# Last channel group, gated values and output products: from weight order over four batches to the order of two batch pairs

## Chip, core and metric

The kernel runs on one core of one Trainium2 chip. The metric is the device time of one execution in microseconds (us). Engines are named as in the profile: PE multiplies matrices, PEld loads their weights, DVE and POOL work on whole tiles, ACT applies functions, SP issues transfers.

## What is computed

Four batches, 448 positions, width 768 (12 heads of 64). Three parts follow each other:

```python
scores = scale * q @ k.T - log(S)
x = sigmoid(scores) @ v                       # attention, heads side by side: (4, 448, 768)

u = x + mix(x)                                # low-rank mixing over positions
y = u + relu(u @ w_ch1) @ w_ch2               # channel products, 768 -> 3072 -> 768

gate_pre[:, s] = sum_k conv_w[k] * y[:, s - 4 + k]    # 5 taps over positions
out = (sigmoid(gate_pre) * (y @ w_val)) @ w_out       # values, then outputs
```

Inputs are fp32, the weights arrive as float64 bits.

## The kernel before

Everything is held transposed: 768 channels are KC = 6 blocks of 128 partitions, and one tile of a batch b and block m is 128 x 448. A product of fp32 precision is made of three matmuls per block of 128 (`mm3`, line 173): weight high x data high, weight high x data low, weight low x data high. So every operand exists as a high part (a copy by ACT) and a low part (a subtraction by DVE or POOL).

The order of instructions on each engine is the order of the program (`tc.manual_schedule`, line 623). Within one engine nothing is passed. Products go through eight PSUM banks in turn.

Weights. There are 120 half weights of 128 x 384: halves 0 to 95 belong to the channel products (twelve groups of eight), 96 to 107 to the six value weights, 108 to 119 to the six output weights. `prep_half` (142) makes the next half ready: four DVE operations unpack the float64 bits (lines 83, 84, 85, 88), one flush later ACT copies the high part (73), and one flush after that DVE subtracts for the low part (75). `prep_half` itself begins with a flush, and so does each product. It also issues the load of the half three later (138, raw ring of three tiles). Prepared halves lie in a pool of ten tiles (`2 * WS`), except for the first three. A product may take its weight in parts: the second half of a weight is first touched by the 10th of 18 matmuls, its low part by the 12th.

Channel groups (570). Group g takes two first products per batch (`ch1`, 371: 18 matmuls, relu by ACT on line 374, low part by DVE on 375) and, per batch and block, one second product (`ch2`, 380: 6 matmuls, added to x by DVE on 387). In the last group `y_split` (389) also splits each finished y: high by ACT (392), low by POOL (393).

Gates (`gate_steps`, 396). Each of the 24 tiles (b, m) goes through five steps: two taps scaled by ACT and added by POOL (410), a third tap scaled by ACT and added by POOL (414), the fourth tap by one DVE operation (417), the fifth by another that writes over y, a sigmoid by ACT (426). `before(i)` and `after(i)` run these steps for several tiles at once, so that each call of the pair moves one tile forward by a step and starts another.

Values (597). For each weight m and each batch b: `val` (429) is a product of 18 matmuls, and DVE multiplies it into the gate (432). After the last weight `z_split` (434) splits the gated tiles: ACT high (73), DVE low (77). An output product `fin` (439, 18 matmuls) needs all six split tiles of its batch; ACT copies it out (441), and SP sends it.

Operand tiles (y, split y, gate, gated and output tiles) share a ring of 32.

By the end of the last group 103 halves are prepared, so seven halves of value weights; ten more follow during the 24 value products, one for every two products.

Of the kernel before, what the change touches and what calls it, by code (L numbers as in the profile page):

```python
# [8 lines left out]
F32 = mybir.dt.float32  # L9
F32R = mybir.dt.float32r  # L10
# [6 lines left out]
P = 128  # L17
B, H, S, D = 4, 12, 448, 64
# [3 lines left out]
KC = DM // P  # L22
NF = DFF // P
G = 2
NG = NF // G
# [4 lines left out]
HQ = DM // 2  # L30
# [2 lines left out]
WS = 5  # L33
LAG = 2
EARLY = 3


@with_exitstack
def tile_kernel(
# [18 lines left out]
    nc = tc.nc  # L58
# [4 lines left out]
    def flush(every=False):  # L63

        while deferred:
            now, deferred[:] = deferred[:], []
            for part in now:
                part()
            if not every:
                return  # L70
# [8 lines left out]
    def unpack(raw, a, x):  # L79


        low, high = raw[:, :, 0], raw[:, :, 1]
        nc.vector.tensor_scalar(a, f32(high), 2.0 ** -112, None, op0=ALU.mult)
        nc.vector.tensor_scalar(x, low, 2.0 ** -29, 7.0, op0=ALU.mult, op1=ALU.min)
        nc.vector.scalar_tensor_tensor(
            x, a.bitcast(U32), 3, x, op0=ALU.logical_shift_left, op1=ALU.bitwise_or
        )
        nc.vector.scalar_tensor_tensor(  # L88
            x, high, 0x80000000, x, op0=ALU.bitwise_and, op1=ALU.bitwise_or
        )  # L90
# [13 lines left out]
    def operand(name, dt=F32R):  # L104
        return op_p.tile([P, 2, S], dt, tag="op", name=name)

    def scratch(name):
        return operand(name, F32)[:, :, :].rearrange("p t s -> p (t s)")
# [5 lines left out]
    def x_of(b, m):  # L114
        return xs[:, m, b, PAD:]
# [7 lines left out]
    pools = {}  # L123
# [5 lines left out]
    def load_half():  # L129
# [3 lines left out]
        n, half = divmod(i, 2)  # L133
        if i < EARLY:
            r = scratch(f"raw{i}")[:, :2 * HQ].bitcast(I64)
# [6 lines left out]
    def prep_half():  # L142
        i = at["prep"]
        if i >= 2 * len(sources):
            return
        flush()
        n, half = divmod(i, 2)
        if i < EARLY:
            t = operand(f"w{i}")[:, :, :HQ]
            ax = operand(f"x{i}", F32)  # L150
            a, x = ax[:, 0, :HQ], ax[:, 1, :HQ].bitcast(U32)
        else:
            t = pools["w"].tile([P, 2, HQ], F32R, tag="w", name=f"w{i}")[:, :, :]
            a = pools["a"].tile([P, HQ], F32, tag="a", name=f"a{i}")[:, :]
            x = pools["a"].tile([P, HQ], U32, tag="x", name=f"x{i}")[:, :]
        wt.setdefault(n, []).append(t)
        unpack(wraw.pop(i), a, x)

        def high():
            split(f32(x), t[:, 0], t[:, 1], later=True)  # L160
            deferred.append(lambda: ready.add(i))

        deferred.append(high)
        at["prep"] += 1
        if i >= EARLY:
            load_half()
# [204 lines left out]
    def ch1(c, b):  # L371
        ps = product(f"ch1_{c}_{b}", weight(c // G * 2 * G + c % G), lambda k: us[b, k])
        t = operand(f"h{c}_{b}")
        nc.scalar.activation(t[:, 0], ps, AF.Relu)  # L374
        nc.vector.scalar_tensor_tensor(  # L375
            t[:, 1], ps, 0.0, f32(t[:, 0]), op0=ALU.max, op1=ALU.subtract
        )
        hs[c, b] = t

    def ch2(g, b, m):  # L380
        flush()
        ws = [weight((2 * g + 1) * G + i) for i in range(G)]
        ps = bank(f"ch2_{g}_{b}_{m}")
        for i in range(G):
            mm3(ps[:, :S], ws[i], m, hs[g * G + i, b], i == 0, i == G - 1)
        y = x_of(b, m)
        nc.vector.tensor_add(y, ps[:, :S], y)  # L387

    def y_split(b, m):
        y = x_of(b, m)  # L390
        t = operand(f"y{b}_{m}")
        nc.scalar.activation(t[:, 0], y, AF.Copy)  # L392
        nc.gpsimd.tensor_sub(t[:, 1], y, f32(t[:, 0]))  # L393
        ys[b, m] = t

    def gate_steps(b, m):

        t = []
        y = xs[:, m, b]
        z = x_of(b, m)  # L400
        tap = lambda k: f32(cw[:, m * TAPS + k:m * TAPS + k + 1])

        def scaled(dst, k):
            nc.scalar.activation(dst, y[:, k:k + S], AF.Copy, scale=tap(k))

        def first():
            t.append(operand(f"g{b}_{m}", F32))
            scaled(t[0][:, 0], 0)
            scaled(t[0][:, 1], 1)
            nc.gpsimd.tensor_add(t[0][:, 0], t[0][:, 0], t[0][:, 1])  # L410

        def second():
            scaled(t[0][:, 1], 2)
            nc.gpsimd.tensor_add(t[0][:, 0], t[0][:, 0], t[0][:, 1])  # L414

        def fused(dst, k):
            nc.vector.scalar_tensor_tensor(
                dst, y[:, k:k + S], tap(k), t[0][:, 0], op0=ALU.mult, op1=ALU.add
            )

        return (
            first,
            second,
            lambda: fused(t[0][:, 0], 3),
            lambda: fused(z, 4),
            lambda: nc.scalar.activation(z, z, AF.Sigmoid),
        )
# [6 lines left out]
    def z_split(b, m):  # L434
        t = operand(f"z{b}_{m}")
        split(x_of(b, m), t[:, 0], t[:, 1])
        zs[b, m] = t
# [29 lines left out]
    def attention_phase(att, kq_scope, raw_scope):  # L467
# [15 lines left out]
        def weights(i):  # L483
            if i < EARLY:
                load_half()
# [37 lines left out]
    def main_phase(tail):  # L523
        mix = iter(tail)

        def take(n):
            for _ in range(n):
                next(mix)()

        flush(every=True)  # L530
        ch1(0, 0)
        take(1)
        settle(0)
        yield
        prep_half()
        ch1(0, 1)
        take(NSC)
        prep_half()
        ch1(0, 2)
        take(1)  # L540
        flush(every=True)
        ch1(1, 0)
        prep_half()
        take(KC)
        flush(every=True)
        ch1(1, 1)
        prep_half()
        prep_half()
        ch1(1, 2)
        prep_half()  # L550
        ch1(0, B - 1)
        ch1(1, B - 1)

        todo = [(b, m) for m in range(KC) for b in range(B)]
        gates = [gate_steps(b, m) for b, m in todo]

        def gate(i, k):
            if 0 <= i < len(gates):
                gates[i][k]()

        def before(i):
            gate(i, 4)
            gate(i + 1, 2)

        def after(i):
            gate(i + 1, 3)
            gate(i + 2, 1)
            gate(i + 3, 0)

        for g in range(NG):  # L570
            n = 2 * G * g
            last = g == NG - 1
            if g == 0:
                flush()
            if g:
                for i in range(G):
                    for b in range(B):
                        ch1(g * G + i, b)
                        if i * B + b < 6:
                            prep_half()  # L580
                    wt.pop(n + i)
            for b in range(B):
                for m in range(KC):
                    ch2(g, b, m)
                    if last:
                        y_split(b, m)
                        if b == B - 1 and m in (2, 3, 4):
                            i = m - 5
                            before(i)
                            after(i)  # L590
                if g == 0 or last or b % 2 == 0:
                    prep_half()
            for i in range(G):
                wt.pop(n + G + i)

        n = 2 * G * NG
        for i, (b, m) in enumerate(todo):
            before(i)
            val(weight(n + m), b, m)
            after(i)  # L600
            if m < KC - 1 and b in (0, 2):
                prep_half()
            if m == KC - 1:
                for k in range(3):
                    z_split(b // 2, 3 * (b % 2) + k)
        n += KC
        for m in range(KC):
            for p in range(2):
                o = operand(f"o{p}_{m}", F32)
                for j in range(2):  # L610
                    b = 2 * p + j
                    fin(weight(n + m), b, m, o[:, j])
                    if m == 0 and b < 2:
                        for k in range(KC):
                            z_split(b + 2, k)
                    if b >= 2:
                        prep_half()
                    if m == KC - 1 and p == 1:
                        nc.sync.dma_start(out[m, :, b], o[:, j])
                if m < KC - 1 or p == 0:  # L620
                    nc.sync.dma_start(out[m, :, 2 * p:2 * p + 2], o)

    with tc.manual_schedule():
        mixc = pool(ctx, "mixc", 1)
# [13 lines left out]
        end = scope()  # L638
# [47 lines left out]
```

## Time and profile before

| what | us |
|---|---|
| median of three runs | 1092.54 |
| lowest, highest | 1091.93, 1094.33 |
| profiled execution, its own time | 1092.42 |
| its span, first to last instruction | 1090.6 |
| PE busy in the span | 1060.4 (97%) |
| DVE busy | 683.1 (63%) |
| ACT busy | 330.8 (30%) |
| POOL busy | 91.9 (8%) |

The span is cut into stretches by what PE does: attention and mixing up to about 200 us, channel groups up to 884.9, values up to 974.4, outputs from 993.4 to 1086.9. A stretch is read by the engine whose end the next one waits for; shares over the whole span hide that POOL works almost only between 858 and 996 us. The granted clock of PE is 1.00 at 2.4 GHz and 0.50 at 1.2 GHz.

### The profile page before, as it was taken

How to read it: one execution, taken by the hardware profiler on the slowest of the kernel's cores; microseconds unless marked ns; L12 is line 12 of the kernel's file. 1: busy time of each engine (PE TensorE's matmuls, PEld its weight loads, DVE VectorE, ACT ScalarE, POOL GpSimd, SP SyncE). 2: the span in 40 equal slices, each digit the busy share in tenths (PEclk: the TensorE clock that was granted, in tenths of full speed). 3: DMA queues.
4: the chain of work that ended last, by engine and by line, in shares of the span. 5: the costliest groups of instructions: out<-in, count | busy, mean ns of one | idle time of the engine just before them, and what ended most of it. 6: DMA issues, size and time to landing. Idle time of an engine off the chain costs nothing.

```text
span 1090.6 us, 13524 instructions
## 1 busy us (share of the span) xinstructions
PE 1060.4 (97%) x5464; PEld 901.5 (83%) x5464; DVE 683.1 (63%) x1247; ACT 330.8 (30%) x565; POOL 91.9 (8%) x77
## 2 busy tenths in 40 slices
PE   8999999999999999999999999999999999975998
PEld 3444446899999999999999999999999999964997
DVE  4454657786666666666566666666656788889510
ACT  5677776302010111111010202020111345557221
POOL 0000000000000000000000000000000485553000
PEclk9999999999999999999999999999999999995999
DMA  6333332213121211212121313121212212110311
GB/s 164 102 103 86 92 104 84 64 53 102 29 73 29 74 44 58 59 44 73 29 73 29 87 29 87 29 73 29 73 44 58 59 30 58 45 44 19 122 68 68
DMA packets 28303, 70.64 MB, mean 65 GB/s; under 512 B 3520, under 2 KB 7216, under 8 KB 28240
## 3 DMA queue, kind: packets, MB, share of 16 engines
q1 hardware_dynamic: 28160, 69.66, 22.5%
q8 instruction: 43, 0.70, 0.3%
q14 instruction: 20, 0.16, 0.1%
q10 hardware_dynamic: 80, 0.11, 0.0%
HBM read 64.26 MB, written 5.51 MB: 64 GB/s over the span
## 4 chain that ended last, share of the span: by engine, by line
PE 88%; POOL 5%; issue 3%; DVE 2%; ACT 0%; DMA 0%; SPq 0%; POOLq 0%; ACTq 0%
PE ch L175 21%; PE ch L177 21%; PE ch L176 21%; PE av L250 7%; PE sc L229 6%; PE fin L176 3%; PE fin L177 3%; PE fin L175 3%; POOL g L414 2%; POOL g L410 2%; PE tr L309 1%; PE pp L323 1%; PE h L345 1%; POOL y L393 1%; DVE z L77 0%
## 5 line engine op out<-in xcount | busy, mean ns | idle before, releaser
L387 DVE TENSOR_TENSOR xs<-ch,xs 128x448 f32<-128x448 f32 x288 | 175.8, 622 | 101.8 <-PE ch L177 101.7
L73 ACT ACTIVATE w<-x 128x384 fp32r<-128x384 f32 x120 | 63.0, 525 | 499.9 <-DVE x L88 496.4
L175 PE MATMUL ch<-u,w 128*128 128x448 f32 x576 | 210.9, 366 | 0.0
L175 PE MATMUL ch<-h,w 128*128 128x448 f32 x576 | 210.6, 366 | 0.0
L176 PE MATMUL ch<-h,w 128*128 128x448 f32 x576 | 210.6, 366 | 0.0
L177 PE MATMUL ch<-h,w 128*128 128x448 f32 x576 | 210.5, 366 | 0.0
L176 PE MATMUL ch<-u,w 128*128 128x448 f32 x576 | 210.5, 365 | 0.0
L177 PE MATMUL ch<-u,w 128*128 128x448 f32 x576 | 210.5, 365 | 0.0
L375 DVE SCALAR_TENSOR_TENSOR h<-ch,h 128x448 fp32r<-128x448 f32 x96 | 59.9, 624 | 133.2 <-ACT h L374 133.2
L175 PEld LDWEIGHTS ch<-u,w 128*128 128x128 f32 x576 | 108.3, 188 | 9.7 <-issue 1.3
L177 PEld LDWEIGHTS ch<-h,w 128*128 128x128 f32 x576 | 108.3, 188 | 8.4
L177 PEld LDWEIGHTS ch<-u,w 128*128 128x128 f32 x576 | 108.3, 188 | 8.4
L175 PEld LDWEIGHTS ch<-h,w 128*128 128x128 f32 x576 | 108.3, 188 | 8.4
L176 PEld LDWEIGHTS ch<-h,w 128*128 128x128 f32 x576 | 108.3, 188 | 8.4
L176 PEld LDWEIGHTS ch<-u,w 128*128 128x128 f32 x576 | 108.4, 188 | 8.3
L393 POOL TENSOR_TENSOR y<-xs,y 128x448 fp32r<-128x448 f32 x24 | 29.0, 1223 | 863.8 <-ACT y L392 863.4
L237 ACT ACTIVATE a<-sc,bias 112x896 f32<-112x896 f32 x96 | 91.5, 1002 | 24.3 <-PE sc L229 23.9
L75 DVE TENSOR_TENSOR w<-x,w 128x384 fp32r<-128x384 f32 x120 | 67.2, 560 | 30.6 <-ACT w L73 29.0
L374 ACT ACTIVATE h<-ch 128x448 fp32r<-128x448 f32 x96 | 51.1, 533 | 109.4 <-PE ch L177 109.3
L250 PE MATMUL av<-a,vr 112*64 112x448 f32 x384 | 82.8, 552 | 0.0
L229 PE MATMUL sc<-ks 64*112 64x448 f32 x576 | 73.4, 387 | 5.1 <-ACT ks L214 5.1
L229 PEld LDWEIGHTS sc<-ks 64*112 64x112 f32 x576 | 48.0, 176 | 30.5 <-ACT a L237 9.4
(75 smaller groups left out, 1183.1 us busy)
## 6 DMA issues: line engine op xcount, KB each, us to landing
raw<-in_w SPq DMA_DIRECT2D x96, 384.0 KB, 3.1
kq<-in_kq SPq DMA_DIRECT2D x47, 224.0 KB, 3.8
vr<-in_va SPq DMA_DIRECT2D x24, 224.0 KB, 2.6
out_t<-o SPq DMA_DIRECT2D x11, 448.0 KB, 2.5
raw<-in_wval SPq DMA_DIRECT2D x12, 384.0 KB, 3.1
raw<-in_wout SPq DMA_DIRECT2D x12, 384.0 KB, 3.2
out_t<-o SPq DMA_DIRECT2D x2, 224.0 KB, 1.9
vraw<-in_v SPq DMA_DIRECT2D x3, 112.0 KB, 3.7
```

Source lines behind the costliest of these rows:

```text
L73: nc.scalar.activation(hi, raw, AF.Copy)
L75: deferred.append(lambda: nc.vector.tensor_sub(lo, raw, f32(hi)))
L175: mm(ps, wk[:, 0], x[:, 0], start=start, stop=False)
L176: mm(ps, wk[:, 0], x[:, 1], start=False, stop=False)
L177: mm(ps, wk[:, 1], x[:, 0], start=False, stop=stop)
L229: mm(ps[:SC, h, :S], ks[r, tk, 0, c * SC:(c + 1) * SC], ks[r, tq, 1], start=t == 0, stop=t == 2,)
L237: nc.scalar.activation(a[:SC], ps[:SC, :, :S], AF.Sigmoid, bias=bias[:SC], scale=1.0 / math.sqrt(D))
L250: mm(ps[D * h:D * h + D, :S], vr[:, h, c], a[:SC, h], start=c == 0, stop=c == NSC - 1,)
L374: nc.scalar.activation(t[:, 0], ps, AF.Relu)
L375: nc.vector.scalar_tensor_tensor(t[:, 1], ps, 0.0, f32(t[:, 0]), op0=ALU.max, op1=ALU.subtract)
L387: nc.vector.tensor_add(y, ps[:, :S], y)
L393: nc.gpsimd.tensor_sub(t[:, 1], y, f32(t[:, 0]))
```

## The change

The last group leaves the loop over groups. It is done for batches 0 and 1 (both first products of each, then second products and splits of y), then for batches 2 and 3. The 24 tiles of gates, values and z splits are listed pair by pair (`todo`), so that all six value weights are used for the first pair and then again for the second. All output products of batches 0 and 1 come ahead of those of 2 and 3.

Gate steps begin earlier: after each of the four first products of the second pair, and twice within its second products, six calls in all before the first value product (three before). z splits of the first pair stand between value products 12 to 19 (two, then one), those of the second pair two at a time behind the first twelve output products.

Weights: four halves are prepared behind the first products of the first pair, two behind the second products of the second pair, so 99 halves by the end of the group. Then one follows each of value products 0 to 8, one each of products 14, 16, 18, 20 and 22, and the rest stand behind output products of the first pair. Since six weights are in use at a time, the last two halves of the value weights and of the output weights (`SPARE`: 106, 107, 118, 119) go into operand tiles.

```diff
+SPARE = [4 * NF + 2 * KC * k - j for k in (1, 2) for j in (1, 2)]
...
+        if i < EARLY or i in SPARE:
+            t = operand(f"w{i}")[:, :, :HQ]
+        else:
+            t = pools["w"].tile([P, 2, HQ], F32R, tag="w", name=f"w{i}")[:, :, :]
...
-        todo = [(b, m) for m in range(KC) for b in range(B)]
+        halves = [range(h, h + B // 2) for h in range(0, B, B // 2)]
+        todo = [(b, m) for bs in halves for m in range(KC) for b in bs]
+        at_gate = [-3]
...
+        def before():
+            gate(at_gate[0], 4)
+            gate(at_gate[0] + 1, 2)
+
+        def after():
+            gate(at_gate[0] + 1, 3)
+            gate(at_gate[0] + 2, 1)
+            gate(at_gate[0] + 3, 0)
+            at_gate[0] += 1
...
-        for g in range(NG):
+        for g in range(NG - 1):
...
+        g = NG - 1
+        for bs in halves:
+            first = bs is halves[0]
+            for i in range(G):
+                for b in bs:
+                    ch1(g * G + i, b)
+                    if first:
+                        prep_half()
+                    else:
+                        before()
+                        after()
+            for b in bs:
+                for m in range(KC):
+                    ch2(g, b, m)
+                    y_split(b, m)
+                    if not first and m == 2:
+                        before()
+                        after()
+                    if not first and m == KC - 1:
+                        prep_half()
...
-        for i, (b, m) in enumerate(todo):
-            before(i)
+        for v, (b, m) in enumerate(todo):
+            second = v >= len(todo) // 2
+            before()
             val(weight(n + m), b, m)
-            after(i)
-            if m < KC - 1 and b in (0, 2):
+            after()
+            if second and len(split_next) > len(todo) // 2:
+                split_some(2 - v % 2)
+            if (v % 2 == 0 and v > len(todo) // 2) or v < 9:
                 prep_half()
-            if m == KC - 1:
-                for k in range(3):
-                    z_split(b // 2, 3 * (b % 2) + k)
         n += KC
-        for m in range(KC):
-            for p in range(2):
-                o = operand(f"o{p}_{m}", F32)
...
+        for bs in halves:
+            for m in range(KC):
+                o = operand(f"o{bs[0]}_{m}", F32)
+                end = bs is halves[-1] and m == KC - 1
+                for j, b in enumerate(bs):
                     fin(weight(n + m), b, m, o[:, j])
...
+                    if bs is halves[0]:
+                        split_some(2)
+                        if m < 2 or j:
+                            prep_half()
+                    if end:
                         nc.sync.dma_start(out[m, :, b], o[:, j])
...
+                if not end:
+                    nc.sync.dma_start(out[m, :, bs[0]:bs[-1] + 1], o)
```

## Rows read from the trace of the kernel before

**Rows 1.** The page's busy times: us, share of the span, instructions.

```profile
PE 1060.4 (97%) x5464; PEld 901.5 (83%) x5464; DVE 683.1 (63%) x1247; ACT 330.8 (30%) x565; POOL 91.9 (8%) x77
```

**Rows 2.** Waits of PE: total us, times, longest.

```profile
PE fin L175 <- ACT z L73: 18.8, 1, 18.8
PE sc L229 <- ACT ks L214: 5.1, 1, 5.1
PE fin L176 <- DVE z L77: 1.4, 2, 0.9
```

**Rows 3.** PE's timeline at stage ends: start, us, operation [idle before, releaser].

```profile
884.87 0.36 PE L175 MATMUL val<-y,w 128*128 128x448 f32 x1
...
974.17 0.37 PE L177 MATMUL val<-y,w 128*128 128x448 f32 x1
993.35 0.74 PE L175 MATMUL fin<-z,w 128*128 128x448 f32 x1 [18.81 <-ACT z L73]
...
1083.81 0.36 PE L175 MATMUL fin<-z,w 128*128 128x448 f32 x1
...
1086.65 0.37 PE L177 MATMUL fin<-z,w 128*128 128x448 f32 x1
```

**Rows 4.** Short stretches: busy PE, PEld, DVE, ACT, POOL, then PEclk, DMA, GB/s.

```profile
979.00:980.00 1.00, 0.00 (x0) 0.00 (x0) 1.00 (x2) 1.00 (x3) 0.42 (x1) 0.83 0.58 98
980.00:981.00 1.00, 0.00 (x0) 0.00 (x0) 0.04 (x1) 1.00 (x3) 1.00 (x1) 0.50 0.77 300
...
1003.00:1004.00 1.00, 1.00 (x5) 0.88 (x5) 1.00 (x3) 1.00 (x4) 0.00 (x0) 0.73 0.03 8
```

**Rows 5.** DVE's timeline around value product 0, the one directly behind another preparation.

```profile
900.51 0.68 DVE L417 SCALAR_TENSOR_TENSOR g<-xs,cw,g 128x448 f32<-128x448 f32 x1
901.11 0.62 DVE L432 TENSOR_TENSOR xs<-val,xs 128x448 f32<-128x448 f32 x1
901.64 0.68 DVE L417 SCALAR_TENSOR_TENSOR xs<-xs,cw,g 128x448 f32<-128x448 f32 x1
902.24 1.51 DVE L75 TENSOR_TENSOR w<-x,w 128x384 fp32r<-128x384 f32 x1
903.67 1.30 DVE L83 TENSOR_SCALAR a<-raw 128x384 f32<-128x384 f32 x1
...
906.35 0.68 DVE L417 SCALAR_TENSOR_TENSOR g<-xs,cw,g 128x448 f32<-128x448 f32 x1
...
910.69 0.55 DVE L75 TENSOR_TENSOR w<-x,w 128x384 fp32r<-128x384 f32 x1
```

**Rows 6.** POOL's timeline beside it.

```profile
901.85 1.48 POOL L414 TENSOR_TENSOR g<-g 128x448 f32<-128x448 f32 x1 [2.27 <-ACT g L404]
903.30 1.46 POOL L410 TENSOR_TENSOR g<-g 128x448 f32<-128x448 f32 x1
```

**Rows 7.** ACT's timeline beside it.

```profile
906.52 0.53 ACT L73 ACTIVATE w<-x 128x384 fp32r<-128x384 f32 x1 [3.16 <-DVE x L88]
```

**Rows 8.** DVE's timeline while POOL splits y without a pause (868.29 to 875.62).

```profile
868.13 2.96 DVE L387 TENSOR_TENSOR xs<-ch,xs 128x448 f32<-128x448 f32 x5
871.01 0.92 DVE L83 TENSOR_SCALAR a<-raw 128x384 f32<-128x384 f32 x1
...
875.96 0.61 DVE L387 TENSOR_TENSOR xs<-ch,xs 128x448 f32<-128x448 f32 x1
```

**Rows 9.** DVE's timeline in the channel group, POOL at rest.

```profile
839.01 0.55 DVE L75 TENSOR_TENSOR w<-x,w 128x384 fp32r<-128x384 f32 x1
839.48 0.35 DVE L83 TENSOR_SCALAR a<-raw 128x384 f32<-128x384 f32 x1
...
840.73 0.56 DVE L88 SCALAR_TENSOR_TENSOR x<-raw,x 128x384 uint32<-128x384 uint32 x1
```

**Rows 10.** DVE's timeline, the loop of two value products: the same operation twice.

```profile
927.19 1.56 DVE L417 SCALAR_TENSOR_TENSOR g<-xs,cw,g 128x448 f32<-128x448 f32 x1 [1.05 <-POOL g L414]
...
936.18 1.56 DVE L417 SCALAR_TENSOR_TENSOR g<-xs,cw,g 128x448 f32<-128x448 f32 x1 [1.05 <-POOL g L414]
```

More of the change, by code (lines that the diff above doesn't have):

```diff
@@ L147, in prep_half @@
         n, half = divmod(i, 2)
+        if i < EARLY or i in SPARE:
+            t = operand(f"w{i}")[:, :, :HQ]
+        else:
+            t = pools["w"].tile([P, 2, HQ], F32R, tag="w", name=f"w{i}")[:, :, :]
         if i < EARLY:
-            t = operand(f"w{i}")[:, :, :HQ]
             ax = operand(f"x{i}", F32)
@@ L152, in prep_half @@
         else:
-            t = pools["w"].tile([P, 2, HQ], F32R, tag="w", name=f"w{i}")[:, :, :]
             a = pools["a"].tile([P, HQ], F32, tag="a", name=f"a{i}")[:, :]
@@ L559, in gate @@
                 gates[i][k]()
[L561 to L568, printed above, removed]
-        for g in range(NG):
+        def before():
[7 more added lines that the diff above has]
+        for g in range(NG - 1):
             n = 2 * G * g
-            last = g == NG - 1
             if g == 0:
@@ L584, in main_phase @@
                     ch2(g, b, m)
[L585 to L588, printed above, removed]
-                            before(i)
-                            after(i)
-                if g == 0 or last or b % 2 == 0:
+                if g == 0 or b % 2 == 0:
                     prep_half()
@@ L594, in main_phase @@
                 wt.pop(n + G + i)
-        n = 2 * G * NG
-        for i, (b, m) in enumerate(todo):
-            before(i)
+        g = NG - 1
[18 more added lines that the diff above has]
+                        prep_half()
@@ L599, in main_phase, with split_some @@
+        n = 2 * G * NG
+        split_next = list(todo)
+        def split_some(count):
+            for _ in range(count):
+                if split_next:
+                    z_split(*split_next.pop(0))
+        for v, (b, m) in enumerate(todo):
+            second = v >= len(todo) // 2
+            before()
             val(weight(n + m), b, m)
-            after(i)
-            if m < KC - 1 and b in (0, 2):
+            after()
+            if second and len(split_next) > len(todo) // 2:
+                split_some(2 - v % 2)
+            if (v % 2 == 0 and v > len(todo) // 2) or v < 9:
@@ L602, in main_phase @@
                 prep_half()
-            if m == KC - 1:
-                for k in range(3):
-                    z_split(b // 2, 3 * (b % 2) + k)
         n += KC
-        for m in range(KC):
-            for p in range(2):
-                o = operand(f"o{p}_{m}", F32)
-                for j in range(2):
-                    b = 2 * p + j
-                    fin(weight(n + m), b, m, o[:, j])
[L613 to L618, printed above, removed]
+        for bs in halves:
[3 more added lines that the diff above has]
+                for j, b in enumerate(bs):
+                    fin(weight(n + m), b, m, o[:, j])
+                    if bs is halves[0]:
[3 more added lines that the diff above has]
+                    if end:
@@ L619, in main_phase @@
                         nc.sync.dma_start(out[m, :, b], o[:, j])
-                if m < KC - 1 or p == 0:
-                    nc.sync.dma_start(out[m, :, 2 * p:2 * p + 2], o)
+                if not end:
+                    nc.sync.dma_start(out[m, :, bs[0]:bs[-1] + 1], o)
     with tc.manual_schedule():
```

## The prediction

> **What bounds the kernel now.** I read the busy line first: PE is busy for 97% of the span [rows 1], so a change can give back only time in which PE stands or runs slowly. The waits of PE say where that is: 18.8 us in one piece before the first output product, which waited for a split gated tile; next come 5.1 us at the start of attention, which the change doesn't touch [rows 2]. PE's timeline puts the piece between 974.5 and 993.35 us [rows 3]. In its middle the granted clock falls from 1.00 to 0.50, and it returns only in the stretch from 1003 us [rows 4].
>
> How much is that in all? Fourteen matmuls run from 1083.81 to 1086.65 [rows 3], so one takes 0.203 us, a product of 18 takes 3.65 us, and 24 products take 87.6 us. Values begin at 884.87 [rows 3]; without any wait they would end at 972.5, where the first output product starts at 993.35: 20.9 us lost. The last matmul ends at 1086.65 + 0.20 = 1086.85, so the outputs take 93.5 us instead of 87.6: 5.9 us lost to the half clock and two short waits. The most that the change can give back is 26.8 us.
>
> Why does PE stand? Two value products take PE 7.3 us, but the loop of gates, products and one preparation on DVE repeats after 936.18 - 927.19 = 8.99 us [rows 10]. DVE, ACT and POOL fall behind, and an output product needs the last of six weights' gated tiles of its batch. This is a wait for throughput of the helpers, not for PE.
>
> **What the change gives.** The order by pairs lets the first outputs need only the first half of the gates, and gates begin three steps earlier. With the twelve gated tiles of the first pair finished at value product 19 and twelve more value products' time in hand for the second, the wait of 18.8 us goes, and with it the clock loss and the gaps behind it. If nothing else became late, 26.8 us would be won.
>
> **What it costs: weights become late.** The order by pairs uses all six value weights in the first twelve products (3.65 x 12 = 43.8 us) instead of in 24. In addition 99 halves are ready by the end of the group, not 103. So nine preparations, halves 99 to 107, follow value products 0 to 8, one each, on the DVE that also does two gate steps and one multiplication per product. Products 2, 4, 6, 8 and 10 each begin a new weight, and the low part of its second half is written one DVE turn before. Nothing hides this: DVE is in order, and PE has no other work in its queue.
>
> *One turn of DVE.* The trace has this turn once: gate step, multiplication, gate step, low part of the last preparation, unpacking of the next, from 900.51 to 906.35: 5.84 us [rows 5]. Alone the same operations take 0.60 + 0.53 + 0.60 [rows 5], 0.47 for the low part and 839.48 to 841.29 = 1.81 for the unpacking [rows 9]: 4.01 us. The difference, 1.83 us, is DVE waiting for POOL's two additions: the low part takes 1.43 instead of 0.47, the first unpacking 1.23 instead of 0.27, while POOL's operations run from 901.85 to 904.76 [rows 5, 6, 9]. Operations with one input from PSUM aren't held: five additions take 2.96 us while POOL never rests [rows 8]. ACT copies the high part 0.17 us after the unpacking ends [rows 5, 7] and only then scales the taps, so POOL's additions fall in the same place of each turn: I take 5.84 for all nine. Bounds: the loop of two products without its idle time and with a second preparation at its price alone (2.28) or held (902.24 to 906.35 = 4.11) gives (8.99 - 1.05 + 2.28) / 2 = 5.11 and (8.99 - 1.05 + 4.11) / 2 = 6.03 [rows 5, 9, 10].
>
> The Trainium skill, page "SBUF — State Buffer", section "SBUF: two separate sides", says that DVE (with two SBUF inputs or in a two-port mode) and GpSimd share a port pair by an exclusive lock, and that the loser is blocked for the other's whole instruction. By that rule with POOL's 1.46 us per addition [rows 6] a turn would be 4.01 + 2 x 1.46 = 6.93. The row shows 0.96 lost per addition, since POOL's 1.46 holds its own wait for DVE.
>
> *When the first turn begins.* Second products of the second pair need 12 x 6 x 0.203 = 14.6 us, so its last first product ends at 884.87 - 14.6 = 870.3. From there DVE does 13 operations with a PSUM input (13 x 0.58 = 7.5 us, by 2.88 us for five [rows 8]), six gate steps, two preparations and one low part, 1.2 us after the product's end for the relu and its hand-over (an estimate from ACT's 0.53 [rows 7] twice). Alone these 15 operations take 6 x 0.60 + 2 x 1.81 + 0.47 = 7.7 [rows 5, 9]: start of turn 0 at 886.7. Held by POOL, an unpacking takes 871.01 to 875.96 = 4.95 [rows 8], so 1.24 per operation and 18.6 in all: 897.6. POOL has 12 y splits and 6 gate additions in this time, 18 x 1.45 = 26 us by its held pace [rows 6], so it hardly rests from 871 to 897, and the upper end is the near one: I take 896.
>
> *The sum.* Nine turns: 896 + 52.6 = 948.6. Behind the last, the low part of half 107 stands after two more gate steps and a multiplication; the same sequence in the trace runs from 906.35 to 910.69 + 0.55 = 4.89 us [rows 5]: 953.45. Product 10 then has seven matmuls left: 954.9. Products 11 to 23 need only PE: 13 x 3.65 = 47.4, so 1002.3; outputs 87.6: 1089.9. That is 3.05 us behind 1086.85. The end after the last matmul (a copy and a transfer) is as before. On the profiled execution, 1092.42 us for a span of 1090.6, this gives 1095.5; the median of the runs, 1092.54, stands 0.1 us beside it.
>
> So the wait moves: 20.9 + 5.9 us go at the outputs, and some 30 us of PE waiting appear within value products 2 to 10, a turn of 5.84 against 3.65, plus the late first turn.
>
> **Edits that cost nothing, and their cover.** The four preparations behind first products of the first pair have a PE product of 3.65 us beside 2.28 of preparation [rows 9]. z splits of the first pair and five preparations between products 12 and 23 make DVE slower than PE for a while (two products: 2 x 2.35 for gates and multiplications, 3.15 for a preparation and 1.6 to 3 for three splits, by the loop's operations [rows 5, 10], against 7.3); by product 19 it is up to 12 us behind, three products, within eight PSUM banks, and nothing is needed from it before the first output at 1002. If that lag doubled, the first output would wait the excess. Loads on SP's queue follow preparations as before, three ahead, so 17 us at this pace. Spare tiles keep preparations from waiting for PE; at no place are all 32 ring tiles in use by my count. The short 0.9 us waits of the outputs go [rows 2].
>
> **Rivals.** (a) *DVE and POOL meet less.* DVE's idle time in the loop [rows 10] shows that turns can slip against POOL. At 5.11 per turn the time is 1095.5 - 9 x 0.73 = 1088.9; from 5.84 - 3.05 / 9 = 5.50 on it is no longer slower than before. Against it: ACT's place in the turn is fixed by the unpacking. (b) *They hardly meet at all.* With 4.01 per turn, turn 0 at 886.7 and a tail without holds (0.60 + 0.53 + 0.60 + 0.60 + 0.47 = 2.8), product 10 ends at 927.0, only 2 us behind the 925.0 of an unbroken PE: 1092.42 - 26.8 + 2.0 = 1067.6. Against it: POOL has its additions to do in just this stretch. (c) *The clock falls.* Before, it fell within 5.5 us of the last matmul [rows 3, 4]. PE will stand for about 4 to 5 us before product 2 and nearly 4 before the last low part, and is busy 7.3 of 11.7 us between. In the middle, DVE's slack of 4.4 us per two products swallows a slow stretch; behind product 10 nothing does. The price is at most 5.9 - 1.4 = 4.5 us [rows 2]: 1100. (d) *Each POOL addition blocks for its whole 1.46 us*, 6.93 per turn: 1105.3; the rule above speaks for it, rows 5 against it. (e) *The order isn't kept*: excluded, since each engine runs the program's order.
>
> **How the numbers follow.** Forecast, 1093.3 to 1098.8: 0.42 (turns of 5.6 to 6.03, turn 0 up to 897.6). (a), 1088 to 1093.3: 0.23. (b), or part of it, 1067 to 1088: 0.09. (c), 1098.8 to 1101.5: 0.20. (d): 0.03; another wait that I haven't seen: 0.03. The range from 1088 to 1101.5 leaves 0.15 out. A measurement of this kernel tells 0.2%, 2.2 us, from no change, so same is 1090.3 to 1094.7. Faster: 0.09 + 0.09 of (a) = 0.18. Same: 0.14 of (a) + 0.12 of the forecast = 0.26. Slower: 0.56.
>
> **What the profile after would show.** Right: no wait of PE before the outputs and a clock of 1.00 there; PE waiting at products 2, 4, 6, 8 and 10 for DVE line 75 and ACT line 73; DVE turns of 5.8 us without idle time from about 896 to 949; product 11 at 955; first output at 1002. Wrong: turns below 5.5, or an unpacking of half 98 done before 890, both of which make it faster; a clock of 0.50 around 950 makes it slower; an output that waits for DVE line 77 would show a lag that I called covered.

## The result and the profile after

The changed kernel takes 1097.47 us, median of five runs from 1097.11 to 1100.29, against 1092.54 before. The ratio is 1.0051, with a 95% interval from 1.0034 to 1.0069: slower by half a per cent, 4.9 us by the medians. The profiled execution took 1097.11 us for a span of 1095.3.

The page's busy times answer to [rows 1]: PE is busy for 6.5 us more and POOL for 3.1 us more, while DVE and ACT do the same work.

```profile
PE 1066.9 (97%) x5464; PEld 903.5 (82%) x5464; DVE 681.7 (62%) x1247; ACT 330.3 (30%) x565; POOL 95.0 (9%) x77
```

PE's waits after (total us, times, longest), to be held against [rows 2]. Line numbers move, those up to 142 by one and later ones by three: line 76 is the low part of a weight, line 74 its high part.

```profile
PE val L180 <- DVE w L76: 13.0, 6, 3.5
PE val L178 <- ACT w L74: 6.4, 4, 3.8
```

The 18.8 us before the outputs are gone. In their place stand ten waits, 19.4 us, all within value products and all for a half weight. The value products that wait are 2, 4, 6, 8 and 10, the ones that begin a new weight. From the first value product (885.38) to the first output (1003.97) PE takes 118.6 us instead of 87.6, 31.0 more: 19.4 us of waits, and 11.6 us in which it restarts or runs slower, mostly at half clock.

PE's timeline at the same places as [rows 3]: the waits before product 2 and within product 10, the first output, the last matmul.

```profile
892.47 0.36 PE L180 MATMUL val<-y,w 128*128 128x448 f32 x1
896.68 0.74 PE L178 MATMUL val<-y,w 128*128 128x448 f32 x1 [3.84 <-ACT w L74]
...
949.67 0.36 PE L179 MATMUL val<-y,w 128*128 128x448 f32 x1
953.56 0.74 PE L180 MATMUL val<-y,w 128*128 128x448 f32 x1 [3.52 <-DVE w L76]
954.10 0.58 PE L178 MATMUL val<-y,w 128*128 128x448 f32 x1
...
1003.97 0.37 PE L178 MATMUL fin<-z,w 128*128 128x448 f32 x1
...
1091.33 0.36 PE L180 MATMUL fin<-z,w 128*128 128x448 f32 x1
```

The outputs now run without any wait or half clock, 87.6 us. But they begin at 1003.97 instead of 993.35.

DVE's timeline in the value stage, from the start of turn 0 to the low part of half 107. To be held against [rows 5]: the same operations in the same order, now nine times.

```profile
895.99 1.55 DVE L420 SCALAR_TENSOR_TENSOR g<-xs,cw,g 128x448 f32<-128x448 f32 x1
...
902.07 0.68 DVE L420 SCALAR_TENSOR_TENSOR g<-xs,cw,g 128x448 f32<-128x448 f32 x1
...
907.87 0.68 DVE L420 SCALAR_TENSOR_TENSOR g<-xs,cw,g 128x448 f32<-128x448 f32 x1
...
909.60 1.51 DVE L76 TENSOR_TENSOR w<-x,w 128x384 fp32r<-128x384 f32 x1
911.03 1.31 DVE L84 TENSOR_SCALAR a<-raw 128x384 f32<-128x384 f32 x1
912.27 0.35 DVE L85 TENSOR_SCALAR x<-raw 128x384 uint32<-128x384 uint32 x1
...
913.72 0.68 DVE L420 SCALAR_TENSOR_TENSOR g<-xs,cw,g 128x448 f32<-128x448 f32 x1
...
948.67 0.68 DVE L420 SCALAR_TENSOR_TENSOR g<-xs,cw,g 128x448 f32<-128x448 f32 x1
...
952.96 0.54 DVE L76 TENSOR_TENSOR w<-x,w 128x384 fp32r<-128x384 f32 x1
```

A turn goes from 907.87 to 913.72, 5.85 us. The low part (909.60) takes 1.43 us to the next start and the first unpacking 1.24, as in [rows 5]. POOL's two additions run just then; the third line below is an addition while DVE stands idle.

```profile
909.15 1.54 POOL L417 TENSOR_TENSOR g<-g 128x448 f32<-128x448 f32 x1 [2.86 <-ACT g L407]
910.66 1.47 POOL L413 TENSOR_TENSOR g<-g 128x448 f32<-128x448 f32 x1
...
954.47 1.14 POOL L413 TENSOR_TENSOR g<-g 128x448 f32<-128x448 f32 x1
```

### The profile page after: what moved, and what is told of

Read it like the earlier page. It is cut to its first block, busy times and chain, and to the rows that moved or that the text cites. A ratio compares the mean times of both kernels' runs of the same rounds, so it can differ in the third digit from the quotient of the medians.

```text
span 1095.3 us, 13504 instructions
## 1 busy us (share of the span) xinstructions
PE 1066.9 (97%) x5464; PEld 903.5 (82%) x5464; DVE 681.7 (62%) x1247; ACT 330.3 (30%) x565; POOL 95.0 (9%) x77
## 4 chain that ended last, share of the span: by engine, by line
PE 92%; DVE 7%; issue 0%; DMA 0%; ACT 0%; POOL 0%; SPq 0%; DVEq 0%; POOLq 0%; ACTq 0%
PE ch L178 21%; PE ch L180 21%; PE ch L179 21%; PE av L253 7%; PE sc L232 6%; PE fin L180 3%; PE fin L178 3%; PE fin L179 3%; PE val L180 2%; PE val L178 2%; PE val L179 2%; DVE w L76 1%; PE tr L312 1%; DVE a L84 1%; DVE g L420 1%; DVE xs L420 1%
## 5 line engine op out<-in xcount | busy, mean ns | idle before, releaser
L76 DVE TENSOR_TENSOR w<-x,w 128x384 fp32r<-128x384 f32 x120 | 76.9, 641 | 8.0 <-ACT w L74 6.2
```

What stands on the lines that cost most here:

```text
L76: deferred.append(lambda: nc.vector.tensor_sub(lo, raw, f32(hi)))
```

## Experiments

Each run stands against runs of the kernel before on the same chip. An edit is to the changed kernel unless another is named. The chips differ a little (the kernel before has medians from 1092.5 to 1093.7 us on them), so a difference between the medians of runs on different chips carries about 1 us of doubt; e1 to e4 ran on one chip, e5 to e8 on another, e9 on a third.

### Is it the preparation? e1_no_preparation

```diff
+    def skip_half():
+        flush()
+        wraw.pop(at["prep"])
+        at["prep"] += 1
+        load_half()
...
-            val(weight(n + m), b, m)
+            val(weight(n), b, m)
...
-            if (v % 2 == 0 and v > len(todo) // 2) or v < 9:
+            if v < 9:
+                skip_half()
+            if v % 2 == 0 and v > len(todo) // 2:
                 prep_half()
```

> The changed kernel with the preparation of halves 99 to 107 left out (their loads stay) and value weight 0 used by all value products. Theory (DVE's turns with a preparation in each pace PE): no wait of PE within the value products, first output product at about 973 us, time 1092.4 - 26.8 = 1066, up to 1068. Rival (the chain of gate steps through ACT, POOL and DVE would hold PE in the pair order even without preparations): PE still waits before or in the outputs, time 1080 or more.

Measured: 1068.44 us, ratio 0.9769 (0.9749 to 0.9789). PE's waits:

```profile
...
PE fin L186 <- DVE w L76: 1.5, 1, 1.5
PE fin L184 <- ACT w L74: 1.0, 1, 1.0
```

Not one wait is left among the value products, and the first output starts at 972.10, where 972.5 was worked out for a PE that never waits. The gates by themselves do keep up in the order by pairs, so the rival falls: the nine preparations are the whole loss of the value stage. (The edit takes out DVE's work and PE's need of the later weights together.) The 2.5 us of waits in the outputs for their own weights make the difference to 1066.

### Is it POOL's share of the turn? e2_no_additions

```diff
             scaled(t[0][:, 0], 0)
             scaled(t[0][:, 1], 1)
-            nc.gpsimd.tensor_add(t[0][:, 0], t[0][:, 0], t[0][:, 1])
...
             scaled(t[0][:, 1], 2)
-            nc.gpsimd.tensor_add(t[0][:, 0], t[0][:, 0], t[0][:, 1])
```

> The changed kernel with POOL's two additions of each gate left out, so two of five taps are missing; POOL keeps the y splits. Theory (POOL's additions hold DVE for 1.8 us per turn): turns of 4.0 us instead of 5.84, turn 0 at 893 to 895, low part of half 107 at about 933, time about 1075. Rival (DVE's turn is long by its own work and by waits for ACT, POOL only fills its gaps): turns of 5.5 us or more, time 1094 to 1097.

Measured: 1074.13 us, ratio 0.9821 (0.9801 to 0.9841). DVE's timeline, turn 0 and the start of turn 1:

```profile
892.97 0.68 DVE L418 SCALAR_TENSOR_TENSOR g<-xs,cw,g 128x448 f32<-128x448 f32 x1
...
894.70 0.55 DVE L76 TENSOR_TENSOR w<-x,w 128x384 fp32r<-128x384 f32 x1
895.16 0.35 DVE L84 TENSOR_SCALAR a<-raw 128x384 f32<-128x384 f32 x1
...
896.89 0.68 DVE L418 SCALAR_TENSOR_TENSOR g<-xs,cw,g 128x448 f32<-128x448 f32 x1
```

The turn is 3.92 us, and DVE's instructions are the same as in the 5.85 us turn. The 1.9 us between them is DVE standing behind two additions of POOL. The Trainium skill, page "SBUF — State Buffer", section "SBUF: two separate sides", gives the rule behind it, an exclusive lock on a port pair; the trace agrees, at 0.96 us lost per addition. It doesn't agree with the 1.46 us that the prediction put on that rule in rival (d): alone, an addition takes POOL 1.14 us (954.47 in the result's rows). DVE's low part starts 0.45 us behind the first of the pair, so it has less than a whole addition to wait for. The longer times of the pair, 1.54 and 1.47, fit POOL's own waits for DVE's operations.

### Does it help to prepare earlier? e3_early, e5_outputs_fed, e6_shorter_lead

e3 moves four preparations ahead:

```diff
                     else:
                         before()
                         after()
+                        if i or b != bs[0]:
+                            prep_half()
...
                     y_split(b, m)
+                    if first and b == bs[0] and m == 2:
+                        prep_half()
...
-            if (v % 2 == 0 and v > len(todo) // 2) or v < 9:
+            if (v % 2 == 0 and v > len(todo) // 2) or v < 5:
                 prep_half()
```

> The changed kernel with four of the nine preparations moved ahead: one behind the third second product of the first pair, one each behind the second, third and fourth first product of the second pair; value products 0 to 4 keep one each. Theory: five turns of 5.84 from about 898, low part of half 107 at about 932, waits of PE only at products 8 and 10, some 8 us in all, time 1074 to 1077. Rival (the moved preparations hold the gates and y splits up by as much, and the lag only changes its place): waits of PE at the second products or at product 2, time 1090 to 1097.

Measured: 1089.96 us, ratio 0.9964 (0.9949 to 0.9978). It is below the kernel before, but 13 us above what I expected. PE's waits:

```profile
PE val L180 <- DVE w L76: 5.4, 2, 3.5
...
PE fin L180 <- DVE w L76: 3.8, 2, 1.9
PE ch L178 <- DVE xs L390: 2.5, 2, 2.1
PE val L178 <- ACT w L74: 2.0, 2, 1.6
PE fin L178 <- ACT w L74: 1.6, 2, 1.0
```

The value products wait for 7.4 us instead of 19.4, as the theory said. But new waits stand on both sides: 2.5 us in the second products, since three preparations among the first products put DVE behind (turn 0 begins at 903.47, not 898), and 5.4 us in the outputs, for output weights. The first output starts at 988.33, 15.6 us earlier than in the changed kernel. DVE's last multiplication of a value, though, comes only 4.8 us earlier, as these two lines show, first of the changed kernel, then of e3:

```profile
1005.65 0.62 DVE L435 TENSOR_TENSOR xs<-val,xs 128x448 f32<-128x448 f32 x1
```

```profile
1000.87 0.62 DVE L435 TENSOR_TENSOR xs<-val,xs 128x448 f32<-128x448 f32 x1
```

So DVE is loaded through the whole value stage. But the waits of the outputs are mostly something else: only the first, 0.55 us, falls before this last multiplication. The other three, 4.8 us, come after it, when DVE has idle time again. Here it waits 1.49 us for ACT's split, and the low part for which PE waits until 1008.57 stands behind:

```profile
1006.88 1.16 DVE L78 TENSOR_TENSOR z<-xs,z 128x448 fp32r<-128x448 f32 x2 [1.49 <-ACT z L74]
1007.96 0.55 DVE L76 TENSOR_TENSOR w<-x,w 128x384 fp32r<-128x384 f32 x1
```

That is the order which e9 changes. The rival of this run was half right: waits at the second products, and a time at the edge of its range.

e5 puts the output stage's preparations behind products 0 to 6:

```diff
-                        if m < 2 or j:
+                        if 2 * m + j < 7:
                             prep_half()
```

> e3_early, and the seven preparations of the output stage follow output products 0 to 6, one each, instead of being spread to product 9. In e3_early PE waited in the outputs for weights: 3.8 + 1.6 us and restarts, some 7 us. Theory: these waits go, the value stage stays as in e3_early, time 1083 to 1084. Rival (DVE has no time for them there either, and the wait only moves): 1088 to 1090.

Measured: 1090.05 us, 0.9976 (0.9963 to 0.9989): nothing gained. The waits of the outputs for the low part rise from 3.8 to 5.7 us, those for the high part (1.6) go, so the sum stays. The theory falls. The rival had the time right, but not its reason: all three waits come after DVE's last multiplication (1001.52), when DVE has idle time.

e6 also leaves out the two calls of gate steps among the second products:

```diff
-                    if not first and m == 2:
-                        before()
-                        after()
```

> e5_outputs_fed without the two calls of gate steps among the second products of the second pair, so that gates run two tiles less ahead; the steps follow later in the same order, where PE bounds. Theory (work of DVE and POOL ahead of turn 0 delays each preparation behind it): turn 0 some 5 us earlier than in e5_outputs_fed, time 1078 to 1080. Rival (gates become late for the first outputs, or the waits before turn 0 are POOL's y splits and not the gates): 1083 or more, with PE waiting for a split gated tile or with turn 0 less than 2 us earlier.

Measured: 1091.94 us, 0.9991 (0.9981 to 1.0000). Turn 0 begins at 899.83 instead of 904.15 in e5, and the first output at 985.26 instead of 989.68. So the work was ahead of turn 0 as the theory had it, but the time missed the theory by 12 us, and the rival's sign is there: in the outputs PE now waits 1.0 us for a split gated tile, and 6.7 us for weights, against 5.7 us in e5. DVE's last multiplication comes at 1002.48, and four of the outputs' seven waits, 4.6 us, fall before it. Steps put off are steps that DVE has to do later.

### What lowers DVE's load? e7_gates_dve, e8_all

e7 takes the additions from POOL and gives them to DVE:

```diff
             scaled(t[0][:, 0], 0)
-            scaled(t[0][:, 1], 1)
-            nc.gpsimd.tensor_add(t[0][:, 0], t[0][:, 0], t[0][:, 1])
 
         def second():
-            scaled(t[0][:, 1], 2)
-            nc.gpsimd.tensor_add(t[0][:, 0], t[0][:, 0], t[0][:, 1])
+            fused(t[0][:, 0], 1)
+            fused(t[0][:, 0], 2)
```

> The changed kernel with POOL's two additions of each gate replaced by DVE: ACT scales the first tap, DVE does each of the other four in one operation that multiplies and adds. Theory (an addition on POOL holds DVE for 0.9 us, longer than the 0.60 us that DVE needs to do it itself): turns of 5.2 us instead of 5.84, low part of half 107 at about 948.5, time 1091 to 1093. Rival (the work put on DVE costs more than the hold that it saves): turns of 5.9 us or more, 1097 to 1103.

Measured: 1096.04 us, 1.0025 (1.0016 to 1.0034). DVE's timeline, turn 0:

```profile
898.71 0.68 DVE L418 SCALAR_TENSOR_TENSOR g<-xs,cw,g 128x448 f32<-128x448 f32 x1
...
900.44 1.40 DVE L418 SCALAR_TENSOR_TENSOR g<-xs,cw,g 128x448 f32<-128x448 f32 x2
901.75 0.55 DVE L76 TENSOR_TENSOR w<-x,w 128x384 fp32r<-128x384 f32 x1
...
903.95 0.68 DVE L418 SCALAR_TENSOR_TENSOR g<-xs,cw,g 128x448 f32<-128x448 f32 x1
```

The turn is 5.24 us, as expected: two more operations on DVE, 1.3 us, cost less than the 1.9 us behind POOL. But turn 0 begins 2.7 us later (898.71), because y splits still run on POOL while DVE does more gates ahead of it, so of the expected 5 us only 1.4 arrived by the medians (2.5 in the profiled executions).

e8 is e6 with this edit.

> e6_shorter_lead with the gates of e7_gates_dve. Theory: both savings add up in part, 1073 to 1076, which would be below both kernels. Rival (DVE is full behind product 12 with two more operations per gate, and the first output waits): PE waits in or before the outputs for DVE, 1080 or more.

Measured: 1083.73 us, 0.9917 (0.9902 to 0.9932). DVE's last multiplication comes at 993.91, and the first output starts at 979.43. That is 8.2 us below e6, where the same edit gave the changed kernel 1.4; in the traces 5.8 us lie ahead of the first output. That a smaller load pays more where the order no longer crowds it into one place is a reading, which no run tests by itself. The time stays above the 1073 to 1076 that I expected, since four waits for low parts, 6.6 us in all, remain in the outputs. By its time and these waits the rival was right; e9 shows that three of them aren't due to a full DVE.

### An order that holds DVE: e9_order

In e8 the low part of a weight stands on DVE behind two z splits, these wait for ACT's high parts, and ACT does them after its copy of the output product that is running. DVE's and ACT's timelines in e8's outputs show it; DVE's idle 1.49 us is no lack of time, and PE waits 1.89 us, until 1011.30, for the low part behind it.

```profile
1006.31 0.35 DVE L84 TENSOR_SCALAR a<-raw 128x384 f32<-128x384 f32 x1
...
1009.61 1.16 DVE L78 TENSOR_TENSOR z<-xs,z 128x448 fp32r<-128x448 f32 x2 [1.49 <-ACT z L74]
1010.69 0.55 DVE L76 TENSOR_TENSOR w<-x,w 128x384 fp32r<-128x384 f32 x1
```

```profile
1008.16 0.53 ACT L74 ACTIVATE w<-x 128x384 fp32r<-128x384 f32 x1 [2.96 <-DVE x L89]
1008.59 0.53 ACT L442 ACTIVATE o<-fin 128x448 f32<-128x448 f32 x1
1009.01 1.03 ACT L74 ACTIVATE z<-xs 128x448 fp32r<-128x448 f32 x2
```

```diff
-                        split_some(2)
                         if 2 * m + j < 7:
                             prep_half()
+                        split_some(2)
```

> e8_all with the preparation behind an output product put ahead of the two z splits instead of behind them. In e8_all PE waits 2.25 us in output products for the low part of a half weight, which stands on DVE behind z splits that wait for ACT's copy of the output product just running. Theory (an order of DVE, not its load): the 2.25 us waits behind products 1, 3, 5 and 7 go, time 1083.7 - 6 = 1077 to 1079. Rival (DVE is full until about 1010 and the weights are late in any order): 1082 to 1084.

Measured: 1075.50 us, 0.9838 (0.9822 to 0.9855). PE's waits:

```profile
PE val L180 <- DVE w L76: 3.0, 1, 3.0
PE fin L178 <- ACT w L74: 1.5, 1, 1.5
...
PE fin L180 <- DVE w L76: 0.9, 1, 0.9
```

Three of the four waits of the outputs for low parts go, and the time falls by 8.2 us (7.3 in the profiled executions); that is more than expected, 1.5 us below the range of the theory. On DVE a preparation and two splits now repeat every 3.27 us (1001.20 to 1004.47), in e8 every 4.85 (1005.84 to 1010.69). This version is faster than both kernels. The same order stands in e3 and e5, with the same 1.49 us of idle time on DVE ahead of the low part, so it fits that more preparations behind the output products couldn't help in e5: each low part stood behind a copy of the product that was to be fed. The swap itself was run only on top of e8.

### What does the half clock cost? e4_filled

```diff
+            wk = w[k // 3][:, :, (k % 3) * P:(k % 3 + 1) * P]
+            if extra and k == KC // 2:
+                mm(ps[:, :S], wk[:, 0], x(k)[:, 0], start=False, stop=False)
+                mm(ps[:, :S], wk[:, 0], x(k)[:, 1], start=False, stop=False)
+                for j in range(extra):
+                    mm(more[:, :S], w[0][:, 0, :P], x(0)[:, 0], start=j == 0, stop=j == extra - 1)
+                mm(ps[:, :S], wk[:, 1], x(k)[:, 0], start=False, stop=False)
...
-        ps = product(f"val{b}_{m}", w, lambda k: ys[b, k])
+        ps = product(f"val{b}_{m}", w, lambda k: ys[b, k], 16 if (b, m) == (0, KC - 1) else 0)
```

Sixteen is the number of extra matmuls in product 10; elsewhere it is zero.

> The changed kernel with sixteen extra matmuls (3.25 us, into a bank that nobody reads) between the 11th and 12th matmul of value product 10, where PE waits 3.5 us. Theory (the half clock behind this wait costs 1.5 us in the profiled execution and more in the runs near 1100): clock 1.00 from 953 to 957, time 1095.5, runs within 1 us of each other. Rival (the clock costs nothing there, the runs differ by something else): 1097.5 or more, with runs near 1100.

Measured: 1095.85 us, 1.0026 (1.0016 to 1.0036). The stretches behind value product 10, first of the changed kernel, then of e4 (busy PE, PEld, DVE, ACT, POOL, then the granted clock, transfers' share, GB/s):

```profile
953.00:954.00 1.00, 0.44 (x1) 0.44 (x2) 0.51 (x2) 1.00 (x3) 0.67 (x1) 0.70 0.00 0
954.00:955.00 1.00, 1.00 (x4) 0.88 (x4) 0.00 (x0) 0.37 (x1) 1.00 (x2) 0.50 0.00 0
955.00:956.00 1.00, 1.00 (x5) 0.88 (x4) 0.00 (x0) 0.00 (x0) 0.61 (x1) 0.50 0.00 0
956.00:957.00 1.00, 1.00 (x5) 0.91 (x4) 0.42 (x1) 0.00 (x0) 0.00 (x0) 0.60 0.06 16
```

```profile
952.00:954.00 2.00, 1.67 (x8) 1.23 (x7) 0.63 (x2) 1.51 (x3) 1.54 (x2) 1.00 0.03 8
954.00:956.00 2.00, 2.00 (x11) 1.81 (x11) 1.57 (x3) 0.32 (x1) 0.75 (x1) 1.00 0.00 0
956.00:958.00 2.00, 2.00 (x12) 1.81 (x11) 0.25 (x1) 1.95 (x4) 1.10 (x1) 1.00 0.00 0
```

The clock stays at 1.00, as the theory has it, and the median falls by 1.6 us, about the 1.5 that the clock costs in the profiled run of the changed kernel (by the ratios, each against the kernel before on its own chip, it falls by 2.7). The intervals of the two ratios overlap (1.0016 to 1.0036 and 1.0034 to 1.0069), so the size is supported rather than settled. That the runs would lie within 1 us was wrong: they reach from 1095.24 to 1098.69, so the rival was right that the runs differ by something else. The last section shows what e4's profile has on that.

## Why the prediction was right, step by step

| step | predicted | measured |
|---|---|---|
| turn 0 of DVE begins | 896 | 895.99 |
| nine turns | 52.6 | 948.67 - 895.99 = 52.7 |
| low part of half 107 done | 953.45 | 952.96 + 0.54 = 953.5 |
| first output | 1002.3 | 1003.97 |
| last matmul ends | 1089.9 | 1091.33 + 0.20 = 1091.5 |
| profiled execution | 1095.5 | 1097.11 |

**What goes.** The wait before the outputs and the clock loss behind it went whole, 26.8 us by the prediction's account. The after trace has neither.

**What comes.** The waits were put at products 2, 4, 6, 8 and 10, for low and high parts of half weights, and they stand there. The price of a turn came from one instance in the trace before [rows 5], and nine of it took 5.85 on the average. That the 1.8 us in it are POOL's was an argument from two held operations [rows 5, 6, 9]; e2 shows it, with a turn of 3.92 when the additions are gone. The bound of 4.01 for a turn without holds was good to 0.1 us. The count behind the start of turn 0 holds too: from 871.57 to 895.99 DVE does just the 13 operations with a PSUM input and the 15 others. That the start came out to 0.01 us is luck: 896 was picked, not worked out, between 886.7 and 897.6. And the "some 30 us of PE waiting" were 31.0 us of lost time, but only 19.4 of them were waits.

**The 1.6 us that were missing** are rival (c), in a smaller size than its price. The matmuls from 953.56 to the first output are 7 + 13 x 18 = 241; at 0.203 us they take 48.9 us, and they took 50.4. The clock was 0.50 from the restart to about 956.7. I had priced the fall at up to 4.5 us, by the outputs before [rows 3, 4]; there the restart was broken by two more waits. In the middle of the value stage the clock fell as well (to 0.50 from 896 to 908 us, to means of 0.69 from 928 to 932 and 0.61 from 940 to 944), and, as the prediction said, DVE's slack covered it: each following low part was later than PE even so. So the forecast and its rival were not cases apart: the fall should have stood in the sum with a price between 0 and 4.5.

**Rivals (a), (b) and (d).** Turns didn't slip against POOL (5.80 to 5.85 from turn 1 on), nor did an addition cost its whole 1.46 us.

**A cover that held for another reason than the one given.** I said that DVE's lag behind product 12 is covered by PE's outputs. In the changed kernel little of the lag was left at the first output, because PE itself was late: DVE's last multiplication is at 1005.65, the first output at 1003.97. With PE earlier the lag stays. In e3 the last multiplication comes 12.5 us behind the first output and in e8 14.5 us, and still no output waits for a gated tile; in e6 it is 17.2 us, and one does, for 1.0 us. So the cover has an end, but it isn't what my expectation for e3 missed by 13 us. There the low part of half 107 was done 5.8 us late, and the outputs took 96.1 us instead of 87.6, more than half of the difference by waits for weights at a time when DVE had idle time.

**Still open.** How much of e9's gain would arrive without e7's edit, with POOL's additions kept, wasn't run.

## What to carry to other kernels

An order that lets a later stage start on half the batches also needs all of its weights in half the time: count the preparations per product of the new order, and price the turn of the engine that makes them from one instance in the trace, holds included. Where the busiest engine waits for another, look whether that other one is full or stands in its order: moving DVE's work about gave 5.5 to 7.5 us over the changed kernel, of some 20 hoped for (e3, e5, e6), and swapping two calls, so that DVE no longer idled 1.49 us for ACT ahead of a weight, gave another 8.2 (e9 against e8). POOL work beside a full DVE isn't free: here an addition on POOL held DVE for 0.96 us, longer than the 0.66 us that DVE took to do it in e7.

## What the hardware showed beyond that

Matmuls of the same shape run at two paces under the same granted clock of 1.00. From 1005 to 1080 us, with PE busy throughout, the changed kernel has 372 matmul records and e4 has 365 (columns as above):

```profile
1005.00:1080.00 75.00, 75.00 (x372) 69.52 (x371) 23.80 (x51) 19.92 (x40) 0.00 (x0) 1.00 0.26 88
```

```profile
1005.00:1080.00 75.00, 75.00 (x365) 68.11 (x364) 22.02 (x47) 19.39 (x39) 0.00 (x0) 1.00 0.25 88
```

By the starts in the timelines the steps are 0.2027 and 0.2066 us, 1.9% apart. In these traces a pace changes only where PE has paused: in the kernel before, 16 matmuls from 970.87 to 974.17 ran at 0.2062, behind a wait of 0.9 us, and the stretch ahead of that wait at 0.2027. In e4 all matmuls from 953 to the end, some 670, ran at the longer step, which is 671 x 0.0039 = 2.6 us. That is the distance between the two groups in which the runs of the changed kernel lie (1097.1 to 1097.5 and 1100.0 to 1100.3), and e4's profiled run, 1097.45, is of e4's own upper group (1097.5 to 1098.7; the lower one is 1095.2 to 1095.9). Group against group, e4 is 1.6 and 1.9 us below the changed kernel, so the pace doesn't account for what e4 gained. That the pace at the last restart makes these groups fits both profiles, but no run set the pace on purpose.
